# Transposing a weight by TensorE between two stages instead of by DMA inside one

## The chip, the cores and the metric

The kernel runs on one core of a Trainium2 chip. The metric is the device time of one execution in microseconds (us). Three runs of the kernel before gave a median of 2164.93 us (2164.41 to 2165.44).

## The reference

Four layers with residual connections on x of 2048 rows by 640 (bfloat16): linear attention A, sliding-window attention B, A, B, where both A layers share one set of weights, and both B layers another. The outputs are the last x and the gradients of x and of the four weights.

```
x = x + A(layernorm(x), A_wqkv, A_wo)     # twice, with B between
A: q, k, v = split(h @ wqkv); phi(t) = where(t > 0, t + 1, exp(t)) + 1e-6
   kv = sum over rows of phi(k) v;  z = sum over rows of phi(k)
   out = (phi(q) @ kv) / (phi(q) . z + 1e-6) @ wo
B: 32 heads of 20, causal window of 256, softmax(q k / sqrt(20)) v @ wo
out, gradients = vjp(x, A_wqkv, A_wo, B_wqkv, B_wo)(grad_out)
```

The gradient with respect to the input of a layer A needs dqkv @ wqkv transposed. The kernel therefore makes a transposed copy of A_wqkv (640 x 1920, "W of layers A") once, and reads it in both backward passes through a layer A.

## The kernel before, in words

Rows are cut into 16 tiles of 128. `forward` (L240) writes the order of the whole forward part out by hand: each helper (`plan_first`, `plan_front`, `plan_rear`, `plan_scores`) gives pairs of a due slot and a function; all pairs are sorted by slot, and the functions issue instructions in that order. The engines PE (TensorE), DVE (VectorE), ACT (ScalarE) and POOL (GpSimd) keep this order exactly, each working through its own queue. DMAs are issued by SP alone, in `dma` (L108, so all of them show as L110); SP's order is chosen by the framework, which may move a DMA ahead of others, except where `behind=True` ties it to the DMA issued before it.

The forward part begins with the **first layer A** (`plan_first`, L580), a row tile every F = 6 slots. For a tile it loads `xi`, normalises it (DVE, one small POOL operation), stores `hn`, transposes hn on PE (`flip`, L158: five 128x128 transposes into one PSUM bank, one copy to SBUF; the copy on ACT shows as L166, the result is `h2T`), and multiplies by the columns of `WA`, held in SBUF, in six products of 128 x 320 (`dense`, L176; all products show as L146). Each of them fills a PSUM bank. For `pk` and `pq` ACT makes an exponential `e` and DVE finishes the feature map from e and the bank (`feature`, L596, shown as L601 and L602); for `v` ACT copies (L618). pk, pq and v are stored to DRAM. The tiles named pk and pq have two buffers each, so that a new one waits for the store of the one before the last. Six small products a tile add phi(k) v into two banks M.

PSUM has five banks in rotation for dense results and flips during this stage (class `Two`, L242, three of one pool and two of another).

After the last tile M is masked (`close_outer`, L199, slot 118) into `mz` and transposed (`turn_outer`, L206, slot 127). The **passage to attention** (slots from about 108 to 138) runs the first tiles of `plan_front` (L453): `pqf` is loaded and flipped, multiplied by mz (`num`), divided into `o`, flipped to `oT`, multiplied by WoA (`proj`), added to xi as `xm`, normalised, flipped to `hnT`, and multiplied by WB (`qkv`). The q, k, v of a tile go to a ring of five SBUF buffers `s`; a DMA transpose writes their turned form `T` of that ring buffer (L527 and L531), and `plan_scores` (L375) multiplies T by T into scores `sT`, the first product of the attention of layer B.

W of layers A is turned during the first layer. `turn(k)` (L300) for k = 0 to 14 issues one DMA transpose of 128 columns of A_wqkv from DRAM to SBUF, 160 KB each, two in every row tile from slot 41.6 on; the results `tw` lie in the space that T will take in the ring's first four buffers. `keep_turned(i)` (L306) stores four of them at a time to `WTAt` in DRAM, where the backward part fetches them. `home(i)` (L310) gives the space to T at slots 96 to 100.

Of the kernel before, what the change touches and what calls it, by code (L numbers as in the profile page):

```python
# [13 lines left out]
BF = mybir.dt.bfloat16  # L14
F32 = mybir.dt.float32
P = 128
D = 640
# [3 lines left out]
T = 2048  # L21
TT = T // P
DT = D // P
G = H // 4
QT = 3 * D
NF = QT // P
# [5 lines left out]
KA = HB * HA  # L32
HALF = H // 2
CW = D // 2
LN_EPS = 1e-5
EPS = 1e-6
CS = float(DH) ** -0.5
# [18 lines left out]
class Kern:  # L56
# [119 lines left out]
    def dense(self, st, lhs, rhs, c0, nk=DT):  # L176
        ps = st.ps.tile([P, 512], F32, name="dense", tag="m")
        for k in range(nk):
            self.mm(ps[:, 0:CW], lhs[:, k, :], rhs[:, k, c0:c0 + CW], k == 0, k == nk - 1)
        return ps  # L180
# [33 lines left out]
    def b_pv(self, st, l, t, g, e, nb, rings, o):  # L214
# [15 lines left out]
        if q == 3:  # L230
            c = g // 4
            r = self.r[l][:, t, c * HALF:(c + 1) * HALF]
            nc.vector.reciprocal(r, st.ops[:, :, DH])
            nc.vector.tensor_tensor(out=self.heads(o[:, c * CW:(c + 1) * CW]), in0=st.ops[:, :, 0:DH],
                                    in1=r.unsqueeze(2).to_broadcast([P, HALF, DH]), op=ALU.mult)
# [4 lines left out]
    def forward(self, st):  # L240
# [8 lines left out]
        nc = self.nc  # L249
# [7 lines left out]
        rings = {i: self.pool(keep if i in (0, 3, 4) else early, f"ring{i}", 1, side="right") for i in (0, 3, 4, 1, 2)}  # L257
# [13 lines left out]
        WA, WoB = vp.tile([P, DT, QT], BF, name="WA"), wo.tile([P, DT, D], BF, name="WoB")  # L271
        WB, WoA = wp.tile([P, DT, QT], BF, name="WB"), wp.tile([P, DT, D], BF, name="WoA")

        def cols(w, kind, c):
            self.dma(w[:, :, c * D:(c + 1) * D], self.W[kind][:, c * D:(c + 1) * D].rearrange("(k p) n -> p k n", p=P))
# [13 lines left out]
        B1, B3, F = 138, 302, 6  # L289
        END = B3 + G * TT  # L290
        plan = []
# [6 lines left out]
        turned = {}  # L298

        def turn(k):  # L300
            i, j = divmod(k, 4)
            if j == 0:
                turned[i] = rings[i].tile([P, 4, D], BF, name=f"tw{i}", tag="T")
            self.dma(turned[i][:, j, :], self.W["A"][:, k * P:(k + 1) * P], transpose=True, behind=True)

        def keep_turned(i):  # L306
            n = min(4, NF - 4 * i)
            self.dma(self.WTA[:, 4 * i * D:(4 * i + n) * D], turned[i][:, 0:n, :].rearrange("p a b -> p (a b)"), behind=True)

        def home(i):  # L310
            st.ring[i]["T"] = rings[i].tile([P, 3, G, P], BF, name=f"T{i}", tag="T")
        plan += [(41.6 + 6 * (k // 2), lambda k=k: turn(k)) for k in range(NF)] + [(57.5 + 12 * i, lambda i=i: keep_turned(i)) for i in range(4)] + [(96 + i, lambda i=i: home(i)) for i in range(5)]
        plan += [(3 + i, lambda c=c: cols(WA, "A", c)) for i, c in enumerate((1, 2, 0))]
        plan += [(40, lambda: square(WoA, "A")), (60, lambda: cols(WB, "B", 1)), (64, lambda: cols(WB, "B", 0)),
                 (70, lambda: cols(WB, "B", 2)), (80, lambda: square(WoB, "B"))]
# [111 lines left out]
    def plan_ln(self, st, l, t, x, src, key, pool):  # L427
# [3 lines left out]
        def stats(c):  # L431
            if c == 0:
                x["bst"] = st.sm.tile([P, 2, 6], F32, name="bst")
            x["st", key] = x.get(("st", key), 0) + 1
            nc.vector.bn_stats(x["bst"][:, c, :], x[src][:, c * CW:(c + 1) * CW])

        def norm():
# [3 lines left out]
            rs = self.rs[l][:, t:t + 1]  # L441
            nc.vector.tensor_scalar(out=rs, in0=mv[:, 1:2], scalar1=LN_EPS, scalar2=None, op0=ALU.add)
            nc.gpsimd.tensor_tensor(out=rs, in0=rs, in1=self.mhalf, op=ALU.pow)
# [9 lines left out]
    def plan_front(self, st, la, lb, t, x, x_in, Wo, W, Wq=None):  # L453
# [14 lines left out]
        def query(c):  # L468
            if c == 0:
                x["pqf"] = st.fb.tile([P, D], BF, name="pqf", bufs=2)  # L470
            self.feature(st, self.dense(st, x["h2T"], Wq, c * CW), x["pqf"][:, c * CW:(c + 1) * CW])()
            if c == 1:
# [5 lines left out]
        def num(c):  # L478
# [5 lines left out]
            for h0, h1, j in ((0, 6, 0), (6, 12, 1), (12, 16, 2)) if c == 0 else ((16, 18, 2), (18, 24, 3), (24, 30, 4), (30, 32, 5)):  # L484
# [5 lines left out]
            nc.vector.reciprocal(r, r)  # L490
            nc.vector.tensor_tensor(out=self.heads(x["o"][:, c * CW:(c + 1) * CW]), in0=ps[:, :, 0:DH],
                                    in1=r.unsqueeze(2).to_broadcast([P, HALF, DH]), op=ALU.mult)
# [8 lines left out]
        def proj(c):  # L501
            if c == 0:
                x["xm"] = st.xm.tile([P, D], BF, name="xm")
            cs = slice(c * CW, (c + 1) * CW)
            ps = self.dense(st, x["oT"], Wo, c * CW)
# [1112 lines left out]
```

## Time and profile before

| | |
|---|---|
| median of three runs | 2164.93 us |
| time of the profiled execution | 2161.81 us |
| its span, first to last instruction | 2160.1 us |
| mean granted clock of TensorE | 0.973 |
| busy: PE, DVE, ACT, POOL | 92%, 63%, 63%, 48% |
| DMA transposes of W (tw) | 15, issued from 32.2 to 74.3 us |
| stores of the turned W (WTAt) | 4, of 640, 640, 640 and 480 KB, issued from 48.0 to 81.5 us |
| last h2T copy of the first layer | 90.09 us |
| first product of scores (sT) | 121.48 us |

Times in the profile are microseconds from the start of the span; the mean of one instruction is in ns. A line of the timeline names start, length, engine, source line, operation, output and input tiles, and count; the bracket behind it is the idle time of the engine before it and what released it. SPq is SP's queue, whose length is the time in which SP is held by issuing; a DMA lands later. Matmuls are pipelined: the time of one, or of a group, includes its way through the array, so the distance to the next group tells what it holds PE for. The granted clock is 1.00 at full speed. A busy share is no bound by itself: what a stage costs is read from what waits there.

### The profile page before, as it was taken

How to read it: one execution, taken by the hardware profiler on the slowest of the kernel's cores; microseconds unless marked ns; L12 is line 12 of the kernel's file. 1: busy time of each engine (PE TensorE's matmuls, PEld its weight loads, DVE VectorE, ACT ScalarE, POOL GpSimd, SP SyncE). 2: the span in 40 equal slices, each digit the busy share in tenths (PEclk: the TensorE clock that was granted, in tenths of full speed). 3: DMA queues.
4: the chain of work that ended last, by engine and by line, in shares of the span. 5: the costliest groups of instructions: out<-in, count | busy, mean ns of one | idle time of the engine just before them, and what ended most of it. 6: DMA issues, size and time to landing. Idle time of an engine off the chain costs nothing. (4 is left out here: it accounts for less than half of the span.)

```text
span 2160.1 us, 76461 instructions
## 1 busy us (share of the span) xinstructions
PE 1990.3 (92%) x32383; PEld 1547.6 (72%) x32383; DVE 1350.9 (63%) x2765; ACT 1362.2 (63%) x1897; POOL 1040.5 (48%) x1663
## 2 busy tenths in 40 slices
PE   7899998799988999999988989989999889999999
PEld 5567776577766877777767868777777678887546
DVE  6788886878754677777746856777777423333001
ACT  5458888378876788888845767888888414332000
POOL 2046666156666457777643455577776401222000
PEclk9999999999998999999998999999999999999999
DMA  9798897589886779999988962799988987999843
GB/s 275 213 222 218 216 216 170 137 213 220 211 212 189 141 161 189 189 191 180 181 238 266 261 193 75 157 189 189 195 179 182 255 271 229 258 223 249 265 120 93
DMA packets 729096, 433.48 MB, mean 201 GB/s; under 512 B 447024, under 2 KB 711344, under 8 KB 728496
## 3 DMA queue, kind: packets, MB, share of 16 engines
q1 hardware_dynamic: 728752, 428.59, 81.2%
q8 instruction: 253, 4.15, 0.8%
q14 instruction: 91, 0.75, 0.1%
HBM read 194.35 MB, written 144.70 MB: 157 GB/s over the span
## 5 line engine op out<-in xcount | busy, mean ns | idle before, releaser
L763 DVE TENSOR_TENSOR ds<-dp,e 128x1024 bf16<-128x1024 f32 (+1 forms) x384 | 443.7, 1155 | 162.6 <-PE s L146 73.3
L759 ACT ACTIVATE e<-s 128x1024 bf16<-128x1024 f32 (+1 forms) x384 | 378.3, 985 | 89.7 <-PE s L146 84.5
L399 ACT ACTIVATE eT<-sT 128x2048 bf16<-128x2048 f32 x180 | 338.0, 1878 | 96.1 <-PE sT L146 84.8
L146 PE MATMUL wg<-rhs,lhs 128*128 128x240 bf16 (+2 forms) x2400 | 334.0, 294 | 9.7 <-DMA lhs<-hn 9.7
L146 PEld LDWEIGHTS <-lhs 128*128 128x128 bf16 x2400 | 232.6, 99 | 86.1 <-DMA lhs<-hn 12.0
L778 POOL TENSOR_SCALAR_AFFINE_SELECT e<-e 128x256 bf16<-128x256 bf16 x512 | 201.6, 409 | 181.8 <-ACT e L759 150.8
L146 PEld LDWEIGHTS <-dqT 128*128 128x128 bf16 x1920 | 169.8, 98 | 65.8 <-issue 8.7
L407 POOL TENSOR_SCALAR_AFFINE_SELECT eT<-eT 128x512 bf16<-128x512 bf16 x256 | 165.0, 648 | 101.4 <-ACT eT L399 101.4
L792 ACT COPY dsT<-flip 128x1024 bf16<-128x1024 bf16 (+1 forms) x200 | 191.2, 956 | 21.9 <-PE flip L787 20.1
L146 PE MATMUL acc<-slabqs,ds 128*128 128x20 bf16 x2880 | 194.6, 172 | 1.7 <-ACT dq L847 1.0
L146 PE MATMUL acc<-ds,e 128*128 128x20 bf16 x2880 | 192.7, 171 | 0.1
L146 PE MATMUL dp<-slabT,dT 32*128 32x128 bf16 (+1 forms) x1952 | 152.1, 245 | 39.2 <-DVE ds L763 33.7
L146 PEld LDWEIGHTS <-ds 128*128 128x128 bf16 x2880 | 176.2, 96 | 10.6 <-issue 6.6
L774 POOL TENSOR_SCALAR_AFFINE_SELECT e<-e 128x512 bf16<-128x512 bf16 x224 | 142.9, 638 | 62.0 <-ACT e L759 59.0
L146 PEld LDWEIGHTS <-e 128*128 128x128 bf16 x2880 | 164.1, 96 | 7.8 <-issue 2.2
L1148 POOL TENSOR_TENSOR dh<-dh,lg 128x640 f32<-128x640 f32 x32 | 46.0, 1438 | 249.6 <-DVE s L1145 241.4
L146 PE MATMUL dense<-WB,hnT 128*128 128x320 bf16 x960 | 161.3, 302 | 0.5 <-DVE s L522 0.3
L146 PE MATMUL dense<-WTA,dqT 128*128 128x320 bf16 x960 | 161.4, 299 | 0.3 <-DVE dqT L1122 0.3
L146 PE MATMUL dense<-WTB,dqT 128*128 128x320 bf16 x960 | 156.3, 302 | 1.9 <-DMA dqT<-dq 1.9
L146 PE MATMUL s<-slabT,slabqT 32*128 32x128 bf16 (+1 forms) x1952 | 147.6, 245 | 6.6 <-ACT e L759 5.6
L410 POOL TENSOR_SCALAR_AFFINE_SELECT eT<-eT 128x512 bf16<-128x512 bf16 x224 | 143.3, 640 | 18.3 <-ACT eT L399 17.1
L787 PE MATMUL flip<-ident,ds 128*128 128x128 bf16 x1824 | 146.9, 222 | 4.2 <-DVE ds L884 4.0
(180 smaller groups left out, 4220.8 us busy)
## 6 DMA issues: line engine op xcount, KB each, us to landing
T<-T SPq DMA_DIRECT2D x96, 256.0 KB, 3.2
rhs<-dqkv SPq DMA_DIRECT2D x40, 480.0 KB, 5.1
s<-s SPq DMA_DIRECT2D x32, 512.0 KB, 3.8
slabT<-T SPq DMA_DIRECT2D x64, 256.0 KB, 4.0
dqkv<-dq SPq DMA_DIRECT2D x16, 960.0 KB, 5.8
dqkv<-dqa SPq DMA_DIRECT2D x32, 480.0 KB, 4.5
rhs<-dqkv SPq DMA_DIRECT2D x12, 960.0 KB, 7.6
hn<-hn SPq DMA_DIRECT2D x64, 160.0 KB, 2.8
```

The source lines that it names most:

```text
L146: return self.nc.tensor.matmul(out, lhsT=lhsT, rhs=rhs, start=start, stop=stop, skip_group_check=True, **kw)
L399: nc.scalar.activation(e, s, ACT.Exp)
L407: nc.gpsimd.affine_select(out=e, in_=e, compare_op=ALU.is_ge, fill=0.0, base=0, pattern=[[0, 4], [1, P]], channel_multiplier=-1)
L410: nc.gpsimd.affine_select(out=e, in_=e, compare_op=ALU.is_ge, fill=0.0, base=-1, pattern=[[0, 4], [-1, P]], channel_multiplier=1)
L759: nc.scalar.activation(u.e[:, :, 0:w], s[:, :, 0:w], ACT.Exp)
L763: nc.vector.tensor_tensor(out=d.ds[:, :, 0:w], in0=d.dp[:, :, 0:w], in1=d.e[:, :, 0:w], op=ALU.mult)
L774: nc.gpsimd.affine_select(out=v, in_=v, pattern=[[0, 4], [1 if far else -1, P]], **kw)
L778: nc.gpsimd.affine_select(out=v, in_=v, pattern=[[0, 2], [1 if far else -1, P]], **kw)
L787: nc.tensor.transpose(ps[:, 4 * j + i, :], f.ds[:, j, i * P:(i + 1) * P], self.ident)
L792: nc.scalar.copy(v(f.dsT), v(ps))
L1148: nc.gpsimd.tensor_tensor(out=x["dh"], in0=x["dh"], in1=L["g"][:, i, :], op=ALU.add)
```

## The change

The turns move out of the first layer and to other engines. `turn(k)` now takes a PSUM bank, transposes five 128x128 blocks of WA (which is in SBUF already) on PE, and copies the bank to tw on ACT. Turns come every 1.5 slots from slot 108 (T0, T1), which is from the last tile's flip of hn into the first tiles of `plan_front`. The stores of WTAt are due some slots after the turn that fills each of them (115, 121, 127 and 131.5), and remain tied to the DMA issued before them. The turned blocks lie in the ring's buffers 4 to 1 instead of 0 to 3, buffer 0 is given to T at slot 106 and the others at slot 132.5. PE has 75 more matrix instructions (with a weight load each) and ACT 15 more copies; SP issues the fifteen transposes no more. The order on DVE and POOL is the same as before, and so is the order of all other instructions of PE and ACT among themselves.

```diff
+T0, T1 = 108, 1.5
...
         def turn(k):
             i, j = divmod(k, 4)
             if j == 0:
-                turned[i] = rings[i].tile([P, 4, D], BF, name=f"tw{i}", tag="T")
-            self.dma(turned[i][:, j, :], self.W["A"][:, k * P:(k + 1) * P], transpose=True, behind=True)
+                turned[i] = rings[4 - i].tile([P, 4, D], BF, name=f"tw{i}", tag="T")
+            tp = st.ps.tile([P, 8, P], BF, name="flip", tag="m")
+            for a in range(DT):
+                nc.tensor.transpose(tp[:, a, :], WA[:, a, k * P:(k + 1) * P], self.ident)
+            nc.scalar.copy(turned[i][:, j, :], tp[:, 0:DT, :].rearrange("p a b -> p (a b)"))
...
-        plan += [(41.6 + 6 * (k // 2), lambda k=k: turn(k)) for k in range(NF)] + [(57.5 + 12 * i, lambda i=i: keep_turned(i)) for i in range(4)] + [(96 + i, lambda i=i: home(i)) for i in range(5)]
+        plan += [(T0 + T1 * k, lambda k=k: turn(k)) for k in range(NF)] + [(T0 + T1 * min(4 * i + 4, NF) + 1, lambda i=i: keep_turned(i)) for i in range(4)]
+        plan += [((B1 - 32 if i == 0 else T0 + T1 * NF + 2), lambda i=i: home(i)) for i in range(5)]
```

## The prediction, as it was recorded

> **What bounds the kernel now.** I read the page first, for the whole span and the slices, then the stretch that the change touches, 0 to 125 us: a windows view cut at the tiles of the first layer, the timeline, the waits, and the tile that the change makes another way.
>
> ```profile
> span 2160.1 us, 76461 instructions
> ...
> PE 1990.3 (92%) x32383; PEld 1547.6 (72%) x32383; DVE 1350.9 (63%) x2765; ACT 1362.2 (63%) x1897; POOL 1040.5 (48%) x1663
> ```
>
> PE is busy 92% of the span, so work that is added to PE is felt unless it falls into one of PE's gaps. The sum is made against this execution's own time, 2161.81 us (span 2160.1); the median of the three runs is 3.12 us above it, and I carry the difference over unchanged. A change under 0.2% (4.3 us) can't be told from none.
>
> The first layer copies one h2T per row tile on ACT, so the distance from one copy to the next is the time of a tile. The windows below are cut at such copies (then at the end of the layer, the start of attention, and a little after).
>
> ```profile
> 49.66:54.35 4.69, 4.69 (x43) 3.59 (x41) 3.69 (x13) 3.17 (x8) 0.55 (x1) 1.00 0.83 190
> 54.35:64.54 10.19, 6.41 (x43) 4.35 (x41) 4.38 (x14) 3.17 (x8) 0.55 (x1) 0.83 0.75 242
> 64.54:90.09 25.55, 23.93 (x207) 17.96 (x205) 19.89 (x66) 15.78 (x36) 2.81 (x5) 1.00 0.97 272
> 89.56:98.28 8.72, 8.24 (x75) 6.15 (x72) 5.62 (x17) 5.34 (x12) 0.00 (x0) 1.00 0.48 156
> 98.28:121.48 23.20, 17.48 (x130) 11.87 (x131) 18.43 (x51) 2.04 (x3) 1.10 (x2) 0.78 0.38 107
> ```
>
> Columns: stretch, length, busy us of PE, PEld, DVE, ACT, POOL, granted clock, DMA share, GB/s. An undisturbed tile takes 4.69 us with PE busy all of it. The next one takes 10.19, a loss of 5.50; the five after it take 25.55 instead of 23.45, a loss of 2.10. Together **7.6 us**. What PE waits for there:
>
> ```profile
> 53.43 0.38 SPq L110 DMA_DIRECT2D pqk<-pk  x1
> 58.18 0.49 DVE L602 SCALAR_TENSOR_TENSOR pk<-dense,e 128x320 bf16<-128x320 f32 x1 [4.13 <-DMA pqk<-pk]
> 58.73 2.83 PE L146 MATMUL dense<-WA,h2T 128*128 128x320 bf16 x10 [3.78 <-DVE pk L602]
> ```
>
> ```profile
> DVE pk L602 <- DMA pqk<-pk: 5.5, 3, 4.1
> PE dense L146 <- DVE pk L602: 4.8, 3, 3.8
> DVE pq L602 <- DMA pqk<-pq: 1.1, 1, 1.1
> ```
>
> The pk tile has two buffers. DVE can't write the next pk until the store of an older one has landed, and that store was issued 4.75 us before. PE stands behind DVE, and then runs ten products in 2.83 us at half clock.
>
> **The change, part by part.** *Removed: fifteen DMA transposes.*
>
> ```profile
> L110 SPq DMA_TRANSPOSE tw<-in_A_wqkv_dram x15: 1167/1259/2209, 32.2 to 74.3; - x15
> L110 SPq DMA_DIRECT2D WTAt<-tw x4: 434/437/456, 48.0 to 81.5; - x4
> ...
> DMA to landing us min/median/max: 3.2/3.8/5.4
> ```
>
> Two transposes a tile hold SP's queue for about 2 x 1.26 = 2.5 us of 4.69, and 2.21 for a single one at worst. A tile's other five issues (xi, pq, pk, v, hn) take about 0.38 each by the pk row above, 1.9. With a WTAt store of 0.44 that is 4.8 us or more of issuing in a tile of 4.69: the queue falls behind, the stores of pk and pq go late, and their buffers come free late. Without them SP issues for 1.9 us a tile. I take the whole loss as gone, **-7.6**; the bounds are -5.5 (the large stall alone) and -7.6, since no tile goes faster than a PE that never idles. What is late next in these tiles is PE itself.
>
> *Added in front of the layer's end: seven of fifteen turns.* A turn is five PE transposes and one ACT copy. By the instruction order of both kernels, turns 0 to 6 stand between the last flip of hn and the flip of pqf, in 89.56 to 98.28, turn 7 before the first num, 8 to 14 up to the second projection of row tile 1.
>
> ```profile
> 89.56 0.44 PE L163 MATMUL flip<-ident,hn 128*128 128x128 bf16 x5
> 89.84 2.20 PE L146 MATMUL dense<-WA,h2T 128*128 128x320 bf16 x15
> 90.09 0.69 ACT L166 COPY h2T<-flip 128x640 bf16<-128x640 bf16 x1
> 97.84 0.44 ACT L600 ACTIVATE e<-dense 128x320 bf16<-128x320 f32 x1 [0.91 <-PE dense L146]
> 98.11 1.00 DVE L203 TENSOR_TENSOR mz<-M,bm 120x378 bf16<-120x378 f32 x2
> ```
>
> The row of the flip says what five transposes cost where PE is pipelined: the next product starts 0.28 us after them. PE was busy 8.24 of 8.72, so 7 x 0.28 = 1.96 is all path. ACT gets 7 x 0.69 = 4.83 on top of 5.34, 10.17 us in a stretch of 8.72 + 1.96 = 10.68: nearly full, so the e and va copies wait behind turns, and the outer product M waits for the last va. I add 0.2 for that: **+2.2**. Bounds: 1.96, and 7 x (0.69 + 0.28) = 6.8 if every turn were passed through in series.
>
> The Trainium skill ("TensorE: Matmul & The Clock Gate", Part 4) puts a 128x128 transpose at some 275 ns in a kernel. An estimate by that page would be 75 x 0.275 = 20.6 us in series, and the kernel 13 us slower; the row's 0.28 for five speaks against it.
>
> *Added in the passage to attention: eight turns.* Here PE has gaps, because DVE (18.43 of 23.20 busy) carries the chain.
>
> ```profile
> 98.70 0.74 PE L146 MATMUL num<-mz,pqT 120*128 120x126 bf16 x7 [0.90 <-DVE mz L203]
> 99.29 0.53 PE L163 MATMUL flip<-ident,pqf 128*120 128x128 bf16 x6
> 100.20 0.29 PE L163 MATMUL flip<-ident,o 128*128 128x128 bf16 x2 [0.39 <-DVE o L491]
> 101.50 0.34 PE L163 MATMUL flip<-ident,o 128*128 128x128 bf16 x3 [1.01 <-DVE o L491]
> 102.42 2.42 PE L146 MATMUL dense<-WoA,oT 128*128 128x320 bf16 x10
> 107.28 0.50 PE L163 MATMUL flip<-ident,o 128*128 128x128 bf16 x3 [1.95 <-DVE o L491]
> 108.21 0.74 PE L163 MATMUL flip<-ident,hn 128*128 128x128 bf16 x5
> 108.74 1.54 PE L146 MATMUL dense<-WoA,oT 128*128 128x320 bf16 x5
> 110.08 0.85 PE L163 MATMUL flip<-ident,pqf 128*120 128x128 bf16 x6
> 112.05 1.39 PE L146 MATMUL dense<-WB,hnT 128*128 128x320 bf16 x5
> ```
>
> Turns 7 (gap 0.90), 8 and 9 (0.39 and 1.01), 11 and 12 (1.95) are covered by these waits for DVE; without the cover each costs 0.28, at half clock 0.56. Turn 10 (between the two projections), 13 (before the flip of hn at 108.21) and 14 (before 110.08) lie on the path: 3 x 0.28 = 0.84, at half clock 1.68. ACT is free there, 2.04 of 23.20, so the copies are hidden.
>
> Against that stands the clock, 0.78 in this stretch:
>
> ```profile
> 55.13:58.54 3.41, 0.00 (x0) 0.00 (x0) 0.36 (x1) 0.32 (x1) 0.00 (x0) 1.00 0.55 176
> 58.54:61.95 3.41, 3.22 (x16) 2.10 (x16) 2.24 (x8) 0.79 (x2) 0.55 (x1) 0.50 0.69 184
> 99.54:102.95 3.41, 1.76 (x17) 1.00 (x16) 3.24 (x11) 0.00 (x0) 0.00 (x0) 0.99 0.43 144
> 102.95:106.36 3.41, 2.39 (x14) 1.34 (x11) 2.73 (x8) 0.00 (x0) 0.00 (x0) 0.50 0.00 0
> 109.78:113.19 3.41, 3.41 (x18) 2.30 (x17) 2.30 (x5) 0.03 (x1) 0.00 (x0) 0.51 0.17 48
> ```
>
> A window in which PE does little is followed by half clock, a full one by full clock. With PE busy 1.76 of 3.41 us the clock fell at 102.95, for 10.2 us. From 107.28 to 112.05 PE does 20 transposes and 10 products, 20 x 0.056 + 10 x 0.136 = 2.5 us at full speed, in 4.77; the five products from 112.05 cost 0.5 too much, and those from 102.42 delay DVE by some 0.6. The half clock costs 2.3 + 0.5 + 0.6 = 3.4. If turns 7 to 9 keep PE busy enough, 3.4 comes back and 0.84 is paid, -2.6; if not, +1.68. PE would be busy some 1.76 + 0.56 = 2.32 of the window, on neither side of what these rows decide, so I take the middle, (-2.6 + 1.7) / 2 = **-0.5**, and keep both ends.
>
> *Moved: the WTAt stores.* Four stores, 0.44 each on SP, now wait for ACT copies, the first before the last v store, the fourth just ahead of the transpose of s for attention's first tile. In 98.28 to 121.48 the DMA share is 0.38, and turn 14's copy is due some 6 us before that transpose (117.00 below), so I cost them at nothing. If the cover is gone, T is late, up to the landing of one store, 3.8.
>
> ```profile
> 117.00 1.36 SPq L110 DMA_TRANSPOSE T<-s  x1
> 121.48 0.40 PE L146 MATMUL sT<-T 32*128 32x128 bf16 x16 [0.80 <-DMA T<-s]
> ```
>
> Sum: -7.6 + 2.2 - 0.5 = -5.9. Profiled 2161.8 - 5.9 = 2155.9; median 2164.9 - 5.9 = **2159.0**. From attention on the instruction order is the same, so the lead should be kept.
>
> **Rivals.** (1) *The clock holds* through the passage: -7.6 + 2.2 - 2.6 = -8.0, 2156.9. For it: the turns fall into PE's gaps. Against: the gap of 1.95 keeps 1.4 even with two turns in it.
>
> (2) *Transposes don't feed the clock*: half clock as before, and turns 10, 13, 14 at double price: -7.6 + 2.2 + 1.7 = -3.7, 2161.2, within 0.2%. For it: in 102.95 to 106.36, with 2.39 us busy, a good part of it flips and small products, the clock stayed at 0.50. Against: a busy share of 0.7 may be too low for any work. The Trainium skill (the same page, Part 4) says that transposes don't count as busy for the gate; by that rule this is the case that comes, 2161.2.
>
> (3) *The stalls were not the transposes' alone*: the 2.1 us of the later tiles stays, or WTAt stores bring such a wait back: -5.5 + 2.2 - 0.5 = -3.8, 2161.1. For it: the DMA share of those tiles is 0.97, and the last transpose is issued at 74.3, long before 90.09. Against: transposes are part of that share, and a queue that is behind needs tiles to catch up.
>
> (4) *ACT's copies become the path, slower than before.* Turns share five PSUM banks with the products; if each of the fifteen holds PE for its copy and its own issue, 0.69 + 0.28 = 0.97, that is 14.6 - 7.6 = +7.0, 2171.9. It decides from 0.51 us a turn (7.6 / 15); over 0.2% slower from 0.80. For it: ACT goes from 61% to nearly full in front. Against: in the passage ACT is idle.
>
> **How the numbers follow.** Forecast 0.45 (own range 2157.3 to 2160.7), rival 1 0.15, 2 0.17, 3 0.11, 4 0.12. Faster by over 0.2% means under 2160.6: 0.37 of the forecast, rival 1, and a little of 2 and 3 if the front costs only 1.96 or less of the passage is paid: 0.56. Within 0.2%: 0.31. Slower: 0.13, rival 4 and a little for a late T. The range leaves out rival 4 and the far side of rival 1: 2155.8 to 2165.5, which holds the lone -5.5 with the half clock (-5.5 + 2.2 + 1.7 = -1.6, 2163.3) and a late T on top of a small gain.
>
> **What would show it.** Right: every tile from 49 to 85 us takes 4.69 and no DVE wait on pqk stores is left; the last h2T copy starts near 82.5; from the last flip of hn to mz it takes 2.2 longer; half clock in the passage is shorter than 10.2 us; attention's first sT starts near 115.6 instead of 121.48. Wrong: waits of pk or pq on DMA stay in the tiles; PE waits for ACT copies of tw; the transpose of s stands behind a WTAt store; or the lead at the first sT is lost later.

## The result and the profile after

| | before | after |
|---|---|---|
| median, in runs taken side by side | 2165.18 us (20 runs, 2157.16 to 2174.12) | 2157.86 us (20 runs, 2151.97 to 2164.21) |
| ratio of times, 95% interval | | 0.9963 (0.9951 to 0.9975) |
| the same, in a second set of runs | 2168.06 us (28 runs) | 2159.52 us (11 runs), 0.9959 (0.9942 to 0.9977) |
| profiled execution | 2161.81 us | 2158.62 us |
| last h2T copy of the first layer | 90.09 us | 82.36 us |
| mz (end of the first layer) | 98.11 us | 91.84 us |
| first sT | 121.48 us | 113.28 us |

The kernel became faster by about 0.4%, 7.3 us by the medians. The forecast was 2159.0, so direction and size came right. Two of its terms missed, by 1.4 and 2.5 us, one of them in the sum and one behind it, in opposite directions. Single executions of one kernel lie up to 17 us apart in the first set, so the 3.2 us between the two profiled executions is not a measure of the change; the stages before attention repeat far better, and they are read from the traces.

The page of the kernel after, with the 75 more PE instructions and the 15 more on ACT:

```profile
span 2156.9 us, 76616 instructions
...
PE 1989.7 (92%) x32458; PEld 1548.7 (72%) x32458; DVE 1352.1 (63%) x2765; ACT 1370.1 (64%) x1912; POOL 1038.4 (48%) x1663
```

The windows of the kernel after, cut as those of before (columns as there): two tiles of the first layer, the five tiles up to the last h2T copy, from turn 0 to the flip of pqf, and on to the first sT; then four single stretches of 3.4 us.

```profile
48.95:53.64 4.69, 4.69 (x43) 3.59 (x41) 3.98 (x14) 3.17 (x8) 0.55 (x1) 1.00 0.53 176
53.64:58.34 4.70, 4.70 (x43) 3.59 (x41) 4.00 (x14) 3.17 (x9) 0.55 (x1) 1.00 0.55 180
58.34:82.36 24.02, 24.02 (x214) 18.36 (x212) 20.49 (x68) 16.41 (x37) 2.74 (x5) 1.00 0.54 177
81.26:91.66 10.40, 10.40 (x111) 8.32 (x109) 5.27 (x16) 8.97 (x18) 0.00 (x0) 1.00 0.49 176
91.66:113.28 21.62, 15.95 (x173) 11.82 (x171) 18.93 (x53) 7.62 (x12) 1.10 (x2) 1.00 0.67 210
...
98.06:101.47 3.41, 1.80 (x34) 1.63 (x32) 2.97 (x10) 1.62 (x3) 0.55 (x1) 1.00 0.37 113
101.47:104.87 3.40, 3.40 (x38) 2.67 (x36) 2.39 (x6) 2.21 (x4) 0.00 (x0) 1.00 0.85 311
121.90:125.30 3.40, 0.37 (x11) 0.33 (x13) 1.78 (x6) 0.00 (x0) 1.16 (x3) 1.00 0.97 280
125.30:128.70 3.40, 3.40 (x33) 2.11 (x33) 1.35 (x5) 1.88 (x1) 0.91 (x2) 0.51 1.13 239
```

Every tile takes 4.69 or 4.70 and PE never idles in these tiles; the last of the five is 5.26 long because turn 0 is in it. The DMA share of the tiles, between 0.75 and 0.97 in before, is about 0.54. In the passage the clock is 1.00 instead of 0.78. The waits of DVE between 25 and 82 us name no store any more:

```profile
DVE e L606 <- ACT e L605: 5.0, 25, 0.2
DVE hn L453 <- POOL rs L448: 2.9, 12, 0.2
```

The timeline of the kernel after, at the points by which the stages are cut, and then that of before where it has not been shown:

```profile
25.49 0.69 ACT L167 COPY h2T<-flip 128x640 bf16<-128x640 bf16 x1
77.10 0.69 ACT L167 COPY h2T<-flip 128x640 bf16<-128x640 bf16 x1
82.36 0.71 ACT L167 COPY h2T<-flip 128x640 bf16<-128x640 bf16 x1
91.84 1.00 DVE L204 TENSOR_TENSOR mz<-M,bm 120x378 bf16<-120x378 f32 x2
113.28 0.40 PE L147 MATMUL sT<-T 32*128 32x128 bf16 x16 [1.13 <-DMA T<-s]
118.64 3.36 SPq L111 DMA_TRANSPOSE T<-s  x1
125.24 0.24 PE L147 MATMUL sT<-T,T 32*128 32x128 bf16 x4 [3.03 <-DMA T<-s]
```

```profile
26.20 0.69 ACT L166 COPY h2T<-flip 128x640 bf16<-128x640 bf16 x1
127.14 2.71 SPq L110 DMA_TRANSPOSE T<-s  x1
131.95 0.24 PE L146 MATMUL sT<-T,T 32*128 32x128 bf16 x4 [1.44 <-DMA T<-s]
```

The lead of the kernel after, point by point, is the difference of the two starts:

| point | lead, us | since the point above |
|---|---|---|
| an early h2T copy (26.20 before) | 0.71 | scatter of the start, before any turn of either kernel |
| last h2T copy | 7.73 | +7.02 |
| mz | 6.27 | -1.46 |
| first sT | 8.20 | +1.93 |
| first sT of tile 1 (131.95 before) | 6.71 | -1.49 |

The tile of 5.26 us holds 0.57 of the turns' price, so the stalls gave 7.02 + 0.57 = 7.59, the front cost 0.57 + 1.46 = 2.03, and the passage gave 1.93: +7.49 up to attention.

### The profile page after: what moved, and what is told of

Same layout as the page of the kernel before. It is cut to its first block, busy times and chain, and to the rows that moved or that the text cites. A ratio compares the mean times of both kernels' runs of the same rounds, so it can differ in the third digit from the quotient of the medians.

```text
span 2156.9 us, 76616 instructions
## 1 busy us (share of the span) xinstructions
PE 1989.7 (92%) x32458; PEld 1548.7 (72%) x32458; DVE 1352.1 (63%) x2765; ACT 1370.1 (64%) x1912; POOL 1038.4 (48%) x1663
```

## Experiments

The theory: fifteen DMA transposes, two in a tile, hold up the stores of the first layer, and without them its stalls go; the turns on PE cost about 0.28 us each where PE is full, and in the passage they pay for themselves, because they keep TensorE's clock up. Its rivals: the stall is one of too few buffers; transposes do not feed the clock, and something else in the changed passage kept it up; the moved stores make a new wait. e1 to e5 are one profiled execution each, which serves for the stages; e6 and the experiments after it were executed 11 or 12 times, beside the kernel before, which gives a ratio to it.

### The turn left out: e1_no_turn, and timed as e9 and e12

```diff
 def keep_turned(i):
-    self.dma(self.WTA[...], turned[i][:, 0:n, :]..., behind=True)
+    self.dma(self.WTA[...], WA.rearrange("p a b -> p (a b)")[...], behind=True)
...
-plan += [(41.6 + 6 * (k // 2), lambda k=k: turn(k)) for k in range(NF)]
```

> The turn is left out altogether: no DMA transposes, no turns on TensorE, and WTAt is stored from WA as it is (so the gradients through layers A are not the reference's). Theory A (the transposes made the waits in the layer, and the added turns keep the clock up in the passage): every tile takes 4.69 us, the last h2T copy comes near 82.1; but the passage falls to half clock for at least two windows (6.8 us) as in the kernel before, and takes 31 us from that copy to the first sT, which comes near 113 to 114, no earlier than with the turns (113.28). Rival B (the clock would have held anyway, and the turns are a plain cost of about 3 us): full clock in the passage, first sT near 110.

> The kernel with no turn at all once more (WTAt stored from WA as it is, so the gradients through layers A are not the reference's), timed. Its lead at the first sT was 10.2 us. If a lead at the first sT is kept to the end, the ratio to before is 0.9953, 10 us. If the later stages take it back, as in its single profile, where it ended 1.7 us after the kernel before's, the ratio is above 0.997.

> The kernel with no turn at all a third time (WTAt stored from WA as it is, so the gradients through layers A are not the reference's). Its lead at 150 us was 9 to 10 us. If leads are kept on average, ratio 0.9955; if the 0.998 of before holds, some 5 us of it are taken back later and the changed kernel can't be judged by its lead in the first stages alone.

The last h2T copy came at 81.52 and the first sT at 111.30, earlier than with the turns. Windows of e1_no_turn, from the last h2T copy on, and its first sT:

```profile
81.52:90.30 8.78, 7.87 (x72) 5.85 (x70) 5.68 (x17) 5.00 (x12) 0.00 (x0) 1.00 0.48 148
90.30:111.30 21.00, 14.99 (x130) 9.94 (x128) 17.67 (x50) 2.04 (x3) 1.10 (x2) 0.92 0.40 112
```

```profile
111.30 0.40 PE L146 MATMUL sT<-T 32*128 32x128 bf16 x16 [0.74 <-DMA T<-s]
```

Counted from the early h2T copy, the first sT came after 86.1, 86.8 and 86.8 us in the three runs, after 87.79 in the kernel after, and 95.28 in before. So the removal is worth 8.5 to 9.2 us there, and the turns on PE cost 1.0 to 1.7 net: against the theory, they do not pay for themselves entirely, since without any turn the half clock was short too (one window of 3.4 us in e1, 6.8 in e9 and e12, against 10.2 in before).

The whole time does not follow: 2163.52 in e1's single execution, 2161.92 in e9 (ratio 0.9980, 0.9965 to 0.9995) and 2163.36 in e12 (0.9975, 0.9957 to 0.9993). With 9 to 10 us of lead at 152 us (by the starts of the same DVE instructions), 4.5 and 4.7 by the medians are left at the end. In all three profiles it loses 2.4 to 3.1 us near 503 us, where a product of scores waits for its T; the waits of PE from 498 to 508 us in e9_no_turn_timed, and then, from 499 to 508, in the kernel after:

```profile
PE sT L146 <- DMA T<-s: 2.5, 1, 2.5
```

```profile
PE sT L147 <- DMA T<-s: 0.4, 1, 0.4
```

That wait (2.5 us here, 2.3 in e1 and in e12) is about half of the 4.5 us that are lost by the medians; it is read from single executions, and the medians need not share it. What decides it was not found.

### Unused transposes put into before: e2_blanks

```diff
+def blank():
+    tp = st.ps.tile([P, 8, P], BF, name="flip", tag="m")
+    for a in range(DT):
+        nc.tensor.transpose(tp[:, a, :], WA[:, a, 0:P], self.ident)
...
+plan += [(118.5 + 1.5 * k, lambda: blank()) for k in range(8)]
```

> The kernel before with its DMA transposes, and eight groups of five TensorE transposes into an unused bank, with no copy, at slots 118.5 to 129, where the changed kernel has its turns 7 to 14. Theory A: the layer loses its 7.6 us as before, but the passage keeps full clock: from the last h2T copy to the first sT about 28.5 to 29 us instead of 31.39. Rival (transposes do not count for the clock): half clock stays as it was, and the three groups on the path add 1.7 us, 33 us.

The window of the passage in e2_blanks, one stretch in it, and its waits of DVE between 25 and 100 us:

```profile
97.90:118.85 20.95, 15.56 (x165) 11.52 (x165) 18.29 (x51) 2.07 (x4) 1.09 (x2) 1.00 0.43 118
...
104.80:108.20 3.40, 1.87 (x27) 1.69 (x28) 2.18 (x8) 1.15 (x2) 0.55 (x1) 1.00 0.45 145
```

```profile
DVE pk L608 <- DMA pqk<-pk: 5.1, 3, 3.8
```

The stalls of the layer are as in before (7.9 us lost). Forty transposes that nobody reads brought the clock of the passage from 0.78 to 1.00, and the time from the last h2T copy to the first sT from 31.39 us to 118.85 - 89.74 = 29.11. More PE work made the stage shorter. This settles rival 2, and the other profiles agree: from the last h2T copy to the first sT the granted clock is 1.00 in all five that have such groups there (after, e2, e6, e10, e13), and 0.84 to 0.94 in the nine that have none.

The size, 2.3 us, is measured against the one profiled execution of before. Of the nine without such groups in the passage it has the longest half clock (10.2 us; the others have 3.4 or 6.8) and takes the longest: they take 29.78 to 31.39 us. Against them e2 is 0.7 to 2.3 us shorter. The whole time, 2169.01 against 2169.8 in one execution each, says nothing at this size.

### The layer: e3_pe_early, e4_three_pk, e5_dma_spread and e11

In e3_pe_early the turns run on PE, but within the layer, at the old slots:

```diff
-plan += [(T0 + T1 * k, lambda k=k: turn(k)) for k in range(NF)]
+plan += [(41.6 + 6 * (k // 2), lambda k=k: turn(k)) for k in range(NF)]
...
```

> The changed kernel with its turns at the old slots, two in each row tile of the layer. Theory A: no wait on a pqk store; a tile with two turns takes 4.69 + 0.56 = 5.25 us, so the last h2T copy comes near 82.1 + 4.2 = 86.3; the passage falls to half clock as in the kernel before, 31 us, and the first sT comes near 117.5, 4 us later than in the changed kernel. If ACT's copies hold PE, a tile takes 4.69 + 2 x 0.97 = 6.6 us and the last copy comes near 96.

The window of a tile with two turns, and then the timeline:

```profile
47.07:52.56 5.49, 5.49 (x54) 4.24 (x52) 4.08 (x13) 4.21 (x10) 0.61 (x1) 1.00 0.61 200
```

```profile
123.00 3.30 SPq L111 DMA_TRANSPOSE T<-s  x1
129.80 0.24 PE L147 MATMUL sT<-T,T 32*128 32x128 bf16 x4 [3.25 <-DMA T<-s]
```

No wait on a store was left, so the stalls go with the DMA transposes wherever the turns are put. Two turns cost a full tile 5.49 - 4.69 = 0.80 us, 0.40 each rather than 0.28: a turn holds PE a little beyond its own issue. The last h2T copy came at 87.19 and the first sT at 117.61, 4.3 later than after. In the passage one window of half clock was left. Its single execution took 2160.36, against 2169.8 of before, which says nothing at this size.

In e4_three_pk the kernel before has three buffers for pk instead of two (and two for h2T, for the space):

```diff
-x[nm] = st.fl.tile([P, D], BF, name=nm, bufs=2)
+x[nm] = st.fl.tile([P, D], BF, name=nm, bufs=3 if nm == "pk" else 2)
```

> The kernel before, DMA transposes and all, with three buffers for pk instead of two (and two for h2T instead of three, to make room). If the two buffers of pk are what turns a late store into a stall, the wait of DVE for the pk store (5.5 us) goes or shrinks to under 2, and the layer loses 2 to 4 us instead of 7.6. Rival: the queue falls further behind with every tile, and a third buffer only puts the stall off: the loss stays at 5 us or more.

The waits of DVE for DMA in e4_three_pk, 25 to 100 us:

```profile
DVE pq L602 <- DMA pqk<-pq: 6.0, 5, 2.5
DVE bst L435 <- DMA xi<-in_A_x_dram: 3.0, 2, 2.0
```

The wait of pk is gone and two others have taken its place; the layer lost 9.4 us instead of 7.6 (the single execution took 2174.99, and the median of before is 2166.4). The pk stores go out as much as 10.1 us after their tile is written, against 9.2 in before, so the queue falls further behind, as the rival had it, and a third buffer for pk only hands the stall on to other tiles. What the buffer taken from h2T did to this was not tested apart.

In e5_dma_spread the DMA transposes stay in the layer, but evenly, one every 4.5 slots from slot 32, where before issues two every 6 slots from 41.6:

```diff
-plan += [(41.6 + 6 * (k // 2), lambda k=k: turn(k)) for k in range(NF)]
+plan += [(32 + 4.5 * k, lambda k=k: turn(k)) for k in range(NF)]
...
```

> The kernel before with its DMA transposes at one per 4.5 slots from slot 32, in place of two per 6 slots from slot 41.6. If the issuing time of SP is the cause (five issues of 0.38, 1.33 transposes of 1.26 and a third of a WTAt store make 3.7 us of 4.69), the queue keeps up and the layer loses under 1 us: last h2T copy at 82 to 83. If the transposes themselves take the DMA engines away from the stores, the loss stays, spread over more tiles: 5 us or more, last copy at 87 or later. The passage falls to half clock in both cases.

> The kernel before with its DMA transposes at one per 4.5 slots, timed. Its lead at 150 us was 3.3 us, with a loss in the layer of 3.9 us instead of 7.6. If leads are kept on average, ratio 0.9985; if the single time of 2157 us was typical, 0.995.

The waits of DVE for DMA in e5_dma_spread, 25 to 100 us, and the issues of the pq stores, with the median time to landing last: e5_dma_spread (25 to 98 us), before (25 to 98) and after (25 to 82).

```profile
DVE pq L602 <- DMA pqk<-pq: 3.2, 6, 0.7
DVE pk L602 <- DMA pqk<-pk: 1.8, 3, 0.8
```

```profile
pqk<-pq SPq DMA_DIRECT2D x15, 160.0 KB, 3.4
```

```profile
pqk<-pq SPq DMA_DIRECT2D x14, 160.0 KB, 3.2
```

```profile
pqk<-pq SPq DMA_DIRECT2D x12, 160.0 KB, 2.0
```

The transposes of e5_dma_spread, with the time that each holds SP in ns (min/median/max):

```profile
L110 SPq DMA_TRANSPOSE tw<-in_A_wqkv_dram x13: 1132/1194/2445, 28.2 to 79.2; - x13
```

A tile has six slots, so it holds 6 / 4.5 = 1.33 transposes, and by the expectation SP issues for 3.7 us in a tile of 4.69. Neither of the two cases came: the layer lost 3.9 us in e5 and 2.1 in e11, in waits of up to 1.0 us. SP's queue is in fact as full as in before. Added up from the timelines, SP issues for 40.3 of the 45 us from 35 to 80 us in before, for 40.4 in e5 and for 39.8 in e11, and its pauses of over 0.3 us come to 0.5 us at most; in after it issues for 18.1. In e5 a transpose held SP for 1.42 us on average, not 1.26, and a load of xi for 0.89, not 0.38.

What the queue does to a store shows in three pk tiles, of before, of e5 and of after. Each fence has DVE's last write into the tile, and then what SP does; the store and the stalled write in before are the rows at 53.43 and 58.18 in the prediction.

```profile
45.94 0.47 DVE L602 SCALAR_TENSOR_TENSOR pk<-dense,e 128x320 bf16<-128x320 f32 x1
49.19 3.51 SPq L110 DMA_TRANSPOSE tw<-in_A_wqkv_dram  x2
```

```profile
55.72 0.47 DVE L602 SCALAR_TENSOR_TENSOR pk<-dense,e 128x320 bf16<-128x320 f32 x1
62.39 0.52 SPq L110 DMA_DIRECT2D pqk<-pk  x1
64.58 0.49 DVE L602 SCALAR_TENSOR_TENSOR pk<-dense,e 128x320 bf16<-128x320 f32 x1 [0.74 <-DMA pqk<-pk]
```

```profile
54.61 0.47 DVE L607 SCALAR_TENSOR_TENSOR pk<-dense,e 128x320 bf16<-128x320 f32 x1
55.11 0.32 SPq L111 DMA_DIRECT2D pqk<-pk  x1
```

In before the store goes out 7.0 us after the tile is written and lands 4.6 us later; in e5 it goes out 6.2 us late and lands in 2.1; in after it goes out 0.03 us late and lands in 1.9. So the stalls of before and of e5 come in the main from stores that stand in SP's queue. Late landings add to them: pq's stores land 1.2 to 1.4 us later beside transposes in the median, by the rows above. At the even pace the delay of a pk store reaches 6.7 us at most in e5 and e11 instead of 9.2, and what it leaves are the short waits. The time is as good as that of the kernel after: 2160.23, ratio 0.9964 (0.9948 to 0.9980).

### Where the turns stand: e6_later, e13_between, e8_second_passage

```diff
-T0, T1 = 108, 1.5
+T0, T1 = 115.6, 1.3   # e6_later
+T0, T1 = 114, 1.15    # e13_between
```

> The changed kernel with its turns from slot 115.6 every 1.3 slots instead of from 108 every 1.5: two turns instead of seven stand in the stretch where PE has no gap, and three or four more fall between the products with WB. If a turn costs what PE pays where it stands (0.28 us in a full stretch, nothing in a gap), five come out of the full stretch (-1.4) and about three go into a nearly full one (+0.8): first sT near 112.7 against 113.28, and the time that of the changed kernel (ratio to before 0.996) within noise. If ACT's copies were what front turns cost, the first sT comes 2 us earlier or more.

> The changed kernel with its turns from slot 114 every 1.15 slots: five instead of seven stand in the full stretch, and the last store of WTAt still comes before attention's first transpose of s, not behind it as with turns from 115.6. From the end of the layer to the first sT this should save about 0.6 to 1.5 us (two turns at 0.28 and some of ACT's queue), so that the first sT comes 30 to 30.5 us after the last h2T copy less turn 0's share; tile 1's wait for T stays at some 3 us if it has nothing to do with the WTAt stores, and grows to 4 if the later stores are its cause. Total: level with the changed kernel (ratio to before 0.995 to 0.997) if leads count; 0.998 or more if, as in the kernels with no turn or with turns elsewhere, a larger early lead is taken back later.

The timelines of e6_later and of e13_between:

```profile
114.39 0.40 PE L147 MATMUL sT<-T 32*128 32x128 bf16 x16 [2.40 <-DMA T<-s]
118.06 0.62 SPq L111 DMA_DIRECT2D WTAt<-tw  x1
121.79 2.28 SPq L111 DMA_TRANSPOSE T<-s  x1
127.27 0.27 PE L147 MATMUL sT<-T,T 32*128 32x128 bf16 x4 [3.95 <-DMA T<-s]
```

```profile
114.68 0.40 PE L147 MATMUL sT<-T 32*128 32x128 bf16 x16 [2.44 <-DMA T<-s]
119.66 2.98 SPq L111 DMA_TRANSPOSE T<-s  x1
124.56 0.24 PE L147 MATMUL sT<-T,T 32*128 32x128 bf16 x4 [0.94 <-DMA T<-s]
```

In e6_later the cover that the prediction spoke of is lost. Its last WTAt store goes out at 118.06, and the turned block in it lies in a ring buffer that T needs next; SP waits for the store to land, as its waits between 115 and 125 us show:

```profile
SPq L111 <- DMA WTAt<-tw: 1.5, 1, 1.5
```

Tile 1's transpose of s comes 3.73 us behind the store, and PE then waits 3.95 for T. The first sT, after a wait of 2.40 for its own T, is later than expected as well (114.39, not 112.7). The kernel is no better than before: 2164.11 against 2166.4, ratio 0.9997 (0.9983 to 1.0011). These waits do not explain the whole of that. By DVE's starts e6 still leads before by 3.7 us at 152 us, where the kernel after leads by 5.8, and e5, which ends as well as after, by 3.3. Where the rest goes was not found.

e13_between stands between the two. Its passage was to become 0.6 to 1.5 us shorter and is no shorter than after's (31.74 against 30.92), tile 1 waits less, and it ends level with the kernel after: 2158.27, ratio 0.9960 (0.9938 to 0.9982).

In e8_second_passage the turns are put behind the forward's second layer, in a place of the same kind, each with a store of its own:

```diff
-T0, T1 = 108, 1.5
+T0, T1 = 276.5, 1.5
...
+tw = st.fl.tile([P, D], BF, name="hn")
...
-nc.scalar.copy(turned[i][:, j, :], tp[:, 0:DT, :]...)
+nc.scalar.copy(tw, tp[:, 0:DT, :]...)
+self.dma(self.WTA[:, k * D:(k + 1) * D], tw)
```

> The changed kernel with its turns in the second passage to attention (slots 276.5 to 297.5, some 370 to 405 us), each into a buffer of its own and stored at once by a DMA of 160 KB. The first layer and passage are then as with no turn at all: first sT near 111.5, 1.7 us before the changed kernel's. In the second passage PE waits for DVE some 8 us, so the turns are hidden except for four or five between products, 1.1 to 1.4 us. If so the kernel is level with the changed one or up to 1 us faster, ratio to before 0.995 to 0.997. Rival: PE's waits there let the clock fall without turns and not with them, and the second passage gets 2 us shorter as well: ratio 0.994 or lower.

Up to attention it ran as the kernel without a turn does (first sT at 112.74). Compared by the starts of the same DVE instructions, its lead over before was 8.9 us ahead of the turns and 5.5 behind them. The other kernels, without turns there, lose 1.0 to 2.8 us of their lead over the same stretch (360 to 415 us), so the turns account for 0.6 to 2.4 of the 3.4. It took 2162.19, ratio 0.9983 (0.9966 to 1.0001): no better place.

### The kernel after once more: e10_after_again

> The changed kernel once more, beside the two below on one chip. In its profile the lead was 8.2 us at the first sT, 5.8 after tile 1 had waited 3.0 us for its T, and 3.2 at the end. If a lead at 150 us is worth its size at the end on average, the ratio to before is 0.9973 (5.8 us) and lies between those of the other two. If the 0.9963 measured first holds again while the kernel with no turn stays at 0.998, something after 150 us favours the changed kernel. Stage times again: last h2T near 82.4, first sT near 113.3.

The window of e10_after_again from the last h2T copy to the first sT:

```profile
81.91:112.83 30.92, 25.25 (x267) 19.24 (x265) 23.10 (x65) 15.70 (x29) 1.09 (x2) 1.00 0.62 199
```

30.92 us, as in the first profile of the kernel after (113.28 - 82.36), at full clock again, and tile 1 waited 2.91 for its T (3.03 there). The stages repeat; the ratio, 0.9959, does too.

## Why the prediction was right, and where it was not

**Layer, -7.6: right,** measured 7.59. All tiles take 4.69, and no store is waited for. The reason given for it, SP overbooked by two transposes a tile, is borne out: before, SP issues for 40.3 us of 45 without a pause worth the name and stores go out up to 9.2 us after their tile is written; after, for 18.1 us, and pk's stores go out 0.03 us after their tile. The working was only too mild. It took 1.26 us for a transpose and 0.38 for each other issue of a tile; from 35 to 80 us they average 1.49 and 0.38 to 0.63. Late landings beside transposes, which it left out, add to the stalls. Rival 3 did not come: nothing of the 2.1 us stayed.

**Front, +2.2: right,** measured 2.03. PE is busy 10.40 of 10.40 us; ACT with 8.97 is less full than the 10.17 foreseen. Rival 4, turns in series with their copies at 0.97 each, is far off: the seven front turns cost 0.29 each, and a turn in a full tile of e3 cost 0.40, both below the 0.51 from which the rival decides. Only the tile with turn 0 grew by more, 0.57: ACT copies the turn ahead of the last h2T there.

**Passage, -0.5: the mis-sized term.** It measured -1.93, and -2.26 without the first sT's longer wait for T (1.13 against 0.80). That is rival 1, -2.6 within 0.4. The size leans on the one profiled execution of before: in the eight other profiles without turns or blanks there, the stretch from the last h2T copy to the first sT takes 0.4 to 1.6 us less than its 31.39. The step that failed was to judge the clock by PE's busy share: "on neither side of what these rows decide", so the middle. The rows after show that this share alone does not decide. A stretch with PE busy 1.80 of 3.41 us was followed by full clock, in before one with 1.76 by half clock, and in e2 one with 1.87 by full clock. What differs in these rows is the count of PE's instructions, 34 and 27 against 17, and the busy time of its weight loads, 1.63 and 1.69 us against 1.00. The stretches need not lie where the gate itself measures, and whether either of the two is what it goes by, no run isolates.

Rival 2 falls by e2 and by both profiles of after: clock 1.00 with turns, 0.78 without them in before. The Trainium skill ("TensorE: Matmul & The Clock Gate", Part 4) says that transposes don't count as busy in the same way and that the full clock doesn't engage for them. Here the clock stays full with them, at 1.00 in five profiles; the measurement decides.

**Moved stores, nothing: right in the sum, wrong behind it.** Up to the first sT no wait for the stores shows. Tile 1's T, however, is late. Its transpose is issued at 118.64 and the product starts at 125.24, 6.60 us later, against 4.81 in before (127.14 to 131.95). PE does 0.37 us of work in the stretch ahead of it and 3.4 us of half clock follow. By DVE's starts, the lead falls from 8.3 at 127 us to 5.8 at 152. It is not the WTAt stores alone, since e3, which made them much earlier, took 6.80 (123.00 to 129.80) and waited 3.25; in e13 the same step took 4.90 (119.66 to 124.56). What makes this one transpose slow in some kernels stays open.

**"The lead should be kept": not one to one.** From 152 us on the profiles of one pair drift apart and together by about 5 us: the kernel after leads by 5.8 at 152 us, by 0.7 at 700, by 4.9 at 1200 and by 0.4 at 1670. The lead of a stage early on does not settle the end. The kernel without a turn led by 9 to 10 us at 152 and ended at 0.9980 and 0.9975; e5 led by 3.3 and e11 by 4.7, and ended as well as after (0.9964); e6 led by 3.7 and ended level with before (0.9997). So the agreement of the total is in part luck. The final -7.3 lies near the lead at the first sT (8.20), two misses, -1.4 in the passage and +2.5 at tile 1's T, cancel in part up to 152 us, and what follows no run explains. That the stages gained what they did is shown; that the 7.3 us at the end are this gain is not.

## What to carry to other kernels

Ask of a DMA transpose in a busy loop what it does to the queue: add up how long each row holds SP, and look how long after its tile a store goes out. An even pace gave the same total here (0.9964) as moving the work to another engine (0.9963), though the queue stayed full. Where an engine has gaps on a chain that is another engine's, work put into them can shorten the stage by holding the clock up, so don't price such work by its own time alone. Keep the moved work's own transfers away from buffers that the next stage needs: with the turns 7.6 slots later, SP stood waiting for one. And don't take a lead in the first stages for the time of the kernel: time it.

## What the runs showed of the hardware

- With eight or more added groups of five TensorE transposes, a stage that runs without them at a granted clock of 0.84 to 0.94 (nine profiles, from the last h2T copy to the first sT) ran at 1.00 (five profiles). Eight groups that nobody reads made it 0.7 to 2.3 us shorter (e2_blanks).
- From 35 to 80 us a DMA transpose of 160 KB held SP for 1.42 to 1.52 us on average (before, e5, e11), an ordinary store of pq or pk for 0.40 to 0.53. With 12 or 13 transposes in these 45 us, SP's queue had no time left, and pk's stores went out up to 9.2 us after their tile was written.
- The pq stores of 160 KB landed in 3.2 to 3.4 us (median) among DMA transposes of the same size (before, e5), and in 2.0 without them (after).
- The DMA transpose of s for tile 1, the same work each time, held SP for 2.28 (e6) to 3.98 us (e5), and took 4.7 (e11) to 6.8 us (e3) from issue to the product that waits for it.
- Single executions of the unchanged kernel lay between 2157.16 and 2174.12 us in the first set, and between 2155.16 and 2181.21 over all sets; a difference of 0.4% was told from none with 20 runs of each kernel.
